# Three one-column constants in one tile: every later buffer 64 bytes lower in a partition

## The chip, the cores and the metric

The kernel runs on one core of one Trainium2 chip. The metric is the device time of one execution in microseconds, as the median of several runs. A core has five engines that take their instructions from queues of their own: TensorE (PE; its weight loads are PEld), VectorE (DVE), ScalarE (ACT), GpSimd (POOL) and SyncE (SP, which here only issues transfers). Transfers between DRAM and the on-chip memory (SBUF, 128 partitions) run on 16 transfer engines that all queues share.

## The reference

One decoding step of a transformer block: attention over a long cache of keys and values for two sequences with one new token each, and then an MLP. All of it is float32.

```python
B, Sq, D = 2, 1, 512
H, Sk, Dh = 32, 8192, 128
def _A_ref(x, k_cache, v_cache, wq, wo):          # caches: (B, H, Sk, Dh)
    q = (x @ wq).reshape(B, Sq, H, Dh).transpose(0, 2, 1, 3)
    scores = jnp.einsum("bhqd,bhkd->bhqk", q, k_cache) * (Dh ** -0.5)
    p = _softmax(scores, axis=-1)
    o = jnp.einsum("bhqk,bhkd->bhqd", p, v_cache)
    return o.transpose(0, 2, 1, 3).reshape(B, Sq, H * Dh) @ wo
def _B_ref(x, w1, b1, w2, b2):                    # w1: (512, 1792)
    y = _layernorm(x, axis=-1)
    h = _gelu(jnp.einsum("bsd,df->bsf", y, w1) + b1)
    return jnp.einsum("bsf,fd->bsd", h, w2) + b2
h = x + _A_ref(_layernorm(x), k_cache, v_cache, wq, wo)
h2 = h + _B_ref(_layernorm(h), w1, b1, w2, b2)
```

Each cache holds 2 x 32 x 8192 x 128 float32 values, 268 MB, and every one of them is read once.

## The kernel before, in words

The 64 pairs of a sequence and a head are taken two heads at a time: 32 iterations `i`, each with one tile of keys and one of values. `load` (L70) brings such a tile, 8 MB, as 128 rows of 64 KB that are contiguous in DRAM, one row to a partition; 64 partitions belong to each of the two heads. The tiles live in the pool `kv`, which has three slots of 64 KB in a partition, so that a load can be issued only when the tile that last used its slot is done with. All these loads, and the weights, are issued on SyncE's queue (L75, L79, L140, L412, L468, L472) in the order of the program.

For the keys of iteration `i`, VectorE multiplies the tile by the query in four chunks of 32 cached positions (`multiply`, L246, in place). The sums over the 128 products are shared out: GpSimd adds the upper half of some positions' products to the lower half (`halve`, L256), VectorE reduces what is left (`sums`, L266), and in the last three iterations ScalarE takes some positions as well (`by_act`, L260). The maximum of the scores (`row_max`, L270) goes through TensorE to all partitions, ScalarE takes the exponentials (`exps`, L291), and TensorE multiplies them by the values of that iteration (`values`, L314) while VectorE is at the keys of the next one. Every second iteration closes two heads: their outputs are summed (`head_sum`, L335), scaled and laid out (`head_out`, L350), and, in groups of rows, multiplied by the output projection, whose rows were loaded into the tile `wog` (`load_wo`, L140, or by an indirect transfer of GpSimd, L145; `turned`, L367). The last two heads' rows of the projection go to `wl`, a view of the query tile `q2` that is free by then (L412).

After the last keys the MLP's weights are loaded into a `kv` slot (`ws`, L468 and L472), w2 in pieces of 7, 4, 2 and 1 rows of 2 KB to a partition; the last values, the rest of the projection, the norm, the MLP and the result follow (L590 and L620 are the MLP's matmuls).

A tile of the `const` pool has its own place in a partition, in the order in which the tiles are made. Each starts at a multiple of 32 bytes, so that a tile with one float32 column takes 32 bytes. The pools `wts` (`wog`), `kv` and `work` lie behind `const` in this order. In the program before, bytes from the start of a partition: `ident` 2176, `orow` 2944, `epst` 7040, `eps2` 7072, `ones` 7104, `onesd` 7616, `ls` 7648, `q2` 11,648, `wog` 15,936, the `kv` slots 24,128, 89,664 and 155,200, the first tile of `work` 220,736; the last ends at 229,312.

`epst` is the bias of the first norm's square root (L197), `eps2` that of the last norm's (L605), and `onesd` holds 1/512, by which a matmul takes the mean of squares (L597).

Of the kernel before, what the change touches and what calls it, by code (L numbers as in the profile page):

```python
# [9 lines left out]
F32 = mybir.dt.float32  # L10
# [6 lines left out]
P = 128  # L17
# [24 lines left out]
def tile_decode_block(ctx: ExitStack, tc: tile.TileContext, x, k, v, wq, wo, w1, b1, w2, b2, out):  # L42
# [14 lines left out]
    const = ctx.enter_context(tc.tile_pool(name="const", bufs=1))  # L57
# [88 lines left out]
            t.rearrange("p r n -> p (r n)"), None, wo_runs, bass.IndirectOffsetOnAxis(index[shut], 0),  # L146
            element_offset=r0 * D, bounds_check=n // r - 1, oob_is_err=False))

    epst = const.tile([P, 1], F32, name="epst")
    nc.vector.memset(epst, EPS)  # L150
    eps2 = const.tile([P, 1], F32, name="eps2")
    nc.vector.memset(eps2, EPS * EPS)
    ones = const.tile([P, P], F32, name="ones")
    nc.vector.memset(ones, 1.0)
    onesd = const.tile([P, 1], F32, name="onesd")
    nc.vector.memset(onesd, 1.0 / D)


# [492 lines left out]
```

## Time and profile before

| what | value |
|---|---|
| median of 3 runs | 1307.6 us (1307.48 to 1307.62) |
| span of the profiled execution, first to last instruction | 1305.9 us (the page gives no other total for it) |
| busy: VectorE, GpSimd, TensorE, ScalarE | 932.7, 494.2, 446.8, 98.6 us |
| read from DRAM | 562.32 MB, 431 GB/s over the span |
| mean granted clock of TensorE | 0.660 |

The page's lines for transfers give, for each queue, the packets, the megabytes, and the time that the packets took as a share of 16 engines' span. A packet here is mostly one contiguous row; 4-byte packets are the signals that a transfer sends when it has landed. The view of windows cuts the span into stretches and gives in its last two columns the share of the 16 transfer engines that packets starting in the stretch took, and GB/s. Where a view says "<-", what stands behind it is what ended the idle time.

### The profile page before, as it was taken

How to read it: one execution, taken by the hardware profiler on the slowest of the kernel's cores; microseconds unless marked ns; L12 is line 12 of the kernel's file. 1: busy time of each engine (PE TensorE's matmuls, PEld its weight loads, DVE VectorE, ACT ScalarE, POOL GpSimd, SP SyncE). 2: the span in 40 equal slices, each digit the busy share in tenths (PEclk: the TensorE clock that was granted, in tenths of full speed). 3: DMA queues.
4: the chain of work that ended last, by engine and by line, in shares of the span. 5: the costliest groups of instructions: out<-in, count | busy, mean ns of one | idle time of the engine just before them, and what ended most of it. 6: DMA issues, size and time to landing. Idle time of an engine off the chain costs nothing.

```text
span 1305.9 us, 7466 instructions
## 1 busy us (share of the span) xinstructions
PE 446.8 (34%) x2934; PEld 130.9 (10%) x2934; DVE 932.7 (71%) x551; ACT 98.6 (8%) x431; POOL 494.2 (38%) x151
## 2 busy tenths in 40 slices
PE   3033313333332334413342232333323334123468
PEld 0001001010010101001010010101001011000113
DVE  3666688757688666787766787666787667797891
ACT  0000000000000000000000000000000000004440
POOL 0433344532344432444332454333444433453330
PEclk9566556766566666656766566666666666566689
DMA  9999999999999999999999999999999999999998
GB/s 418 426 440 428 438 422 444 424 440 426 442 426 440 428 438 428 426 444 430 436 426 438 430 434 436 424 442 424 440 426 432 438 432 436 429 428 429 428 434 351
DMA packets 12727, 561.50 MB, mean 430 GB/s; under 512 B 1568, under 2 KB 1584, under 8 KB 2484
## 3 DMA queue, kind: packets, MB, share of 16 engines
q1 hardware_dynamic: 11968, 557.08, 98.8%
q0 software_dynamic: 720, 3.93, 0.7%
q8 instruction: 23, 0.38, 0.1%
q14 instruction: 12, 0.10, 0.0%
q10 hardware_dynamic: 4, 0.00, 0.0%
HBM read 562.32 MB, written 0.00 MB: 431 GB/s over the span
## 4 chain that ended last, share of the span: by engine, by line
DMA 43%; DVE 24%; issue 14%; PE 12%; POOL 5%; ACT 1%; SPq 0%; POOLq 0%; DVEq 0%
DMA kv<-in_A_k_cache_dram 38%; DVE kv L246 14%; PE so L314 10%; DVE s L266 9%; POOL kv L256 5%; DMA kv<-in_A_v_cache_dram 3%; DMA ws<-in_B_w_dram 1%; ACT pt L291 1%; PE rowacc L367 1%; DVE orow L350 1%; PE sm L280 1%; PE sm L273 0%; DVE gm L277 0%; DVE mx L270 0%; ACT nb L286 0%
## 5 line engine op out<-in xcount | busy, mean ns | idle before, releaser
L246 DVE TENSOR_TENSOR kv<-kv,qps 128x4096 f32<-128x4096 f32 x128 | 562.4, 4415 | 313.8 <-DMA kv<-in_A_k_cache_dram 313.6
L256 POOL TENSOR_TENSOR kv<-kv 128x2048 f32<-128x2048 f32 (+3 forms) x128 | 476.8, 3734 | 754.1 <-DVE kv L246 566.3
L266 DVE TENSOR_REDUCE s<-kv 128x32 f32<-128x2048 f32 (+5 forms) x160 | 325.3, 2066 | 10.9 <-POOL kv L256 10.6
L314 PE MATMUL so<-kv,pt 128*8 128x512 f32 x2048 | 280.8, 709 | 42.7 <-ACT pt L291 37.3
L273 PE MATMUL sm<-ident,mx 128*1 128x128 f32 x32 | 10.9, 340 | 446.0 <-DVE mx L270 446.0
L314 PEld LDWEIGHTS so<-kv,pt 128*8 128x8 f32 x2048 | 56.4, 101 | 239.5 <-issue 194.3
L367 PE MATMUL rowacc<-wog,ot 128*2 128x512 f32 x70 | 50.3, 881 | 64.8 <-DVE ot L365 33.4
L286 ACT ACTIVATE nb<-sm 128x2 f32<-128x2 f32 x32 | 5.5, 172 | 851.4 <-PE sm L280 851.4
L231 PE MATMUL qps<-q,pick 2*64 2x256 f32 x64 | 13.8, 577 | 127.6 <-DVE kv L246 127.6
L273 PEld LDWEIGHTS sm<-ident,mx 128*1 128x1 f32 x32 | 2.5, 79 | 472.5 <-issue 278.0
L358 PE MATMUL sm<-ident,orow 2*128 2x2 f32 x35 | 5.2, 244 | 130.1 <-DVE orow L350 130.1
L320 ACT ACTIVATE ss<-so 128x512 f32<-128x512 f32 x31 | 18.5, 598 | 269.6 <-PE so L314 269.6
L260 ACT ACTIVATE kv<-kv 128x128 f32<-128x128 f32 x114 | 33.5, 295 | 24.2 <-DVE kv L246 21.4
L335 PE MATMUL sm<-ss,selr 128*34 128x128 f32 x240 | 28.7, 273 | 0.0
L291 ACT ACTIVATE pt<-s,nb 64x128 f32<-64x128 f32 x64 | 25.5, 399 | 1.4
L335 PEld LDWEIGHTS sm<-ss,selr 128*34 128x34 f32 x240 | 25.1, 112 | 0.0
L260 ACT ACTIVATION_READ_ACCUMULATOR kv<-kv 128x1 f32 x114 | 21.3, 186 | 0.0
L280 PE MATMUL sm<-gm,ones 1*128 1x2 f32 x64 | 16.6, 326 | 11.9 <-DVE gm L277 11.9
L277 DVE TENSOR_REDUCE gm<-sm 1x2 f32<-1x128 f32 x32 | 8.9, 279 | 16.2 <-PE sm L273 16.2
L231 PEld LDWEIGHTS qps<-q,pick 2*64 2x64 f32 x64 | 5.5, 192 | 136.9 <-DVE kv L246 133.2
L358 PEld LDWEIGHTS sm<-ident,orow 2*128 2x128 f32 x35 | 4.4, 207 | 132.6 <-DVE orow L350 79.9
L367 PEld LDWEIGHTS rowacc<-wog,ot 128*2 128x2 f32 x70 | 6.8, 107 | 97.9 <-issue 64.1
(110 smaller groups left out, 169.2 us busy)
## 6 DMA issues: line engine op xcount, KB each, us to landing
kv<-in_A_k_cache_dram SPq DMA_DIRECT2D x4, 4096.0 KB, 32.9
ws<-in_B_w_dram SPq DMA_DIRECT2D x3, 1792.0 KB, 18.5
kv<-in_A_v_cache_dram SPq DMA_DIRECT2D x1, 4096.0 KB, 33.4
wog<-in_A_wo_dram SPq DMA_DIRECT2D x3, 1024.0 KB
kv<-in_A_v_cache_dram SPq DMA_DIRECT2D x1, 2048.0 KB, 37.9
kv<-in_A_v_cache_dram SPq DMA_DIRECT2D x1, 1536.0 KB, 41.2
ws<-in_B_w_dram SPq DMA_DIRECT2D x1, 1024.0 KB, 17.0
wog<-in_A_wo_dram SPq DMA_DIRECT2D x1, 512.0 KB
```

The source lines that it names most:

```text
L231: nc.tensor.matmul(t[e * HP:(e + 1) * HP, :, b], pick[32 * n:32 * n + B, b, :], rows[:, :, e], start=True, stop=True)
L246: return nc.vector.tensor_tensor(kc, kc, qb, op=ALU.mult)
L256: nc.gpsimd.tensor_tensor(t[:, :, :DH // 2], t[:, :, :DH // 2], t[:, :, DH // 2:], op=ALU.add)
L260: nc.scalar.activation(kt[i][:, j, :], kt[i][:, j, :], AF.Copy, accum_out=ST[i][:, j:j + 1])
L266: nc.vector.tensor_reduce(ST[i][:, a:e], kt[i][:, a:e, :d], axis=AX.X, op=ALU.add)
L273: nc.tensor.transpose(MT[i], mx, ident)
L280: GI[i] = nc.tensor.matmul(GM[i], ones[:1, :], gm, start=True, stop=True)
L291: nc.scalar.activation(ptz[i % 2][ps, :, 4 * e:4 * e + 4], s[ps], AF.Exp, bias=nb[ps, e:e + 1], scale=SCALE, accum_out=LT[m][ps, 32 * e + ...
L314: m = nc.tensor.matmul(so[32 * n:32 * n + 4 * QG], ptz[i % 2][:, u, :], vt[i][:, 4 * u:4 * u + 4, :], start=(u < NG), stop=(u >= NS // 4 - ...
L320: return nc.scalar.activation(SS[i], so2[i % 2], AF.Copy)
L335: nc.tensor.matmul(OP[m], sel_row[:, j, B - 1 - c:B - 1 - c + QR], SS[i - 1 + c][:, j * DH:(j + 1) * DH], start=(c == 0 and j == 0), stop= ...
L367: nc.tensor.matmul(rowacc, t[:, r, :], wo_g[g][:, r, :], start=False, stop=(g == len(groups) - 1 and r == n - 1))
```

## The change

The three tiles `epst`, `eps2` and `onesd` of one column each become the three columns of one tile `small`. The memsets that fill them, and their readers, are as before. By the rule of 32 bytes for a tile, `small` takes 32 bytes where the three took 96. `ones`, which stood between the second and the third, moves 32 bytes down, and all that is made after `onesd`, with the pools behind `const`, moves 64 bytes down.

```diff
-    epst = const.tile([P, 1], F32, name="epst")
+    small = const.tile([P, 3], F32, name="small")
+    epst, eps2, onesd = (small[:, j:j + 1] for j in range(3))
     nc.vector.memset(epst, EPS)
-    eps2 = const.tile([P, 1], F32, name="eps2")
     nc.vector.memset(eps2, EPS * EPS)
     ones = const.tile([P, P], F32, name="ones")
     nc.vector.memset(ones, 1.0)
-    onesd = const.tile([P, 1], F32, name="onesd")
     nc.vector.memset(onesd, 1.0 / D)
```

## The prediction

> **What bounds the kernel now.** I read the page from its busy shares to its transfers, then the queue of the loads, then the chain at the end.
>
> ```profile
> span 1305.9 us, 7466 instructions
> PE 446.8 (34%) x2934; PEld 130.9 (10%) x2934; DVE 932.7 (71%) x551; ACT 98.6 (8%) x431; POOL 494.2 (38%) x151
> DMA  9999999999999999999999999999999999999998
> ...
> DMA packets 12727, 561.50 MB, mean 430 GB/s; under 512 B 1568, under 2 KB 1584, under 8 KB 2484
> ...
> q1 hardware_dynamic: 11968, 557.08, 98.8%
> q0 software_dynamic: 720, 3.93, 0.7%
> q8 instruction: 23, 0.38, 0.1%
> ...
> kv<-in_A_v_cache_dram SPq DMA_DIRECT2D x31, 30.6
> kv<-in_A_k_cache_dram SPq DMA_DIRECT2D x30, 38.4
> ```
>
> No engine is above 71%, but the transfers are: the shares of the queues add up to 98.8 + 0.7 + 0.1 = 99.6% of 16 transfer engines' span, or 1300.7 us of 1305.9. The next rows, stretches of the windows view (the last two columns are the transfers' share and GB/s), show where the rest is: ahead of the first load and behind the last.
>
> ```profile
> 0.00:1.80 1.80, 0.00 (x0) 0.00 (x0) 0.79 (x1) 0.49 (x1) 1.22 (x9) 1.00 0.43 148
> 1.80:1302.00 1300.20, 445.90 (x2918) 130.57 (x2922) 931.67 (x550) 98.08 (x431) 492.93 (x143) 0.66 1.00 432
> 1302.00:1305.90 3.90, 0.86 (x24) 0.33 (x16) 0.29 (x1) 0.00 (x0) 0.00 (x0) 0.88 0.00 1
> ```
>
> Between 1.8 and 1302 us the transfers never rest. The queue is never short of a load either: one is released when the scores' maximum or the last value matmul gives a buffer back, as the waits of SyncE's queue show, and the V loads then take 30.6 us to land.
>
> ```profile
> SPq L75 <- DVE mx L270: 764.5, 28, 29.7
> SPq L75 <- PE sm L301: 175.9, 15, 12.6
> SPq L75 <- PE so L314: 170.4, 15, 13.3
> ```
>
> What a load needs by itself is worked out below (19.4 us). So a V load is issued 30.6 - 19.4 = 11.2 us before its transfer can begin, a K load 38.4 - 19.4 = 19.0 us. That much delay of the computing costs nothing. The chain at the end is transfers too, from the value loads' issue until 1301.75 us, with 1.2 us of computing after that before the result is sent:
>
> ```profile
> 1242.83 42.02 DMA kv<-in_A_v_cache_dram
> 1284.85 0.02 issue
> 1284.87 16.88 DMA ws<-in_B_w_dram
> 1301.75 0.04 issue
> 1301.79 0.64 PE po L620 x16
> ```
>
> So the time is the start, plus bytes and packets through 16 engines, plus a short end. The page gives the profiled execution a span of 1305.9 us and no total of its own; the median of the runs is 1307.6, 1.7 us above the span. I take those 1.7 us as lying around the span and carry them over unchanged.
>
> **The price of a transfer.** To see what an address can change I need the part of a transfer that is not proportional to its bytes. Two rows give it: the page's whole q1 row above (mostly rows of 64 KB), and the last weight pieces, 2 KB and 4 KB rows (1297 to 1302 us). A third window holds two 4-byte packets and nothing else.
>
> ```profile
> q1 hardware_dynamic: 410, 1.63, 80.2%
> ```
>
> ```profile
> q0 software_dynamic: 2, 0.00, 5.6%
> ```
>
> Let a packet cost a, and a kilobyte (1000 B) on one engine b. The whole: 11968 a + 557,080 b = 0.988 x 16 x 1305.9 us = 20,644 us. The small pieces: 410 a + 1630 b = 0.802 x 16 x 5 us = 64.2 us. That gives a = 10.0 ns (give or take 0.5 ns for the rounded megabytes) and b = 36.84 ns, or 27.1 GB/s on an engine and 434 GB/s on 16. A 64 KB row (65.5 x 36.84 + 10) is 2424 ns, and a load of eight rows per engine 19.4 us. As a sum over the kernel: 561.50 MB x 36.84 / 16 = 1292.9 us for bytes and 12,727 x 10.0 / 16 = 8.0 us for packets, together 1300.9 against 1300.7 in the shares. A stretch that was not used fits:
>
> ```profile
> DMA packets 7773, 390.84 MB, mean 433 GB/s; under 512 B 988, under 2 KB 988, under 8 KB 1244
> ...
> q1 hardware_dynamic: 7175, 387.39, 99.2%
> ```
>
> This is 297 to 1200 us: 7175 x 0.010 + 387.39 x 36.84 = 14,343 us by the two prices, 0.992 x 16 x 903 = 14,332 by the row.
>
> The third window is 0.02 us long: 0.056 x 16 x 20 ns = 18 ns for two packets, 9 ns for one of 4 bytes. A packet too small to straddle any boundary thus pays nine tenths of what a 64 KB row pays beyond its bytes.
>
> [...]
>
> **The change part by part.** *The three memsets* stay, with the same shapes and places in the program, and so do the readers of the three columns:
>
> ```profile
> 1.87 0.06 DVE L150 MEMSET epst<- 128x1 f32 x1
> 1.88 0.06 DVE L152 MEMSET eps<- 128x1 f32 x1
> 2.03 0.06 DVE L156 MEMSET onesd<- 128x1 f32 x1
> 4.59 0.29 ACT L197 ACTIVATE lnsd<-lnmv,epst 2x1 f32<-2x1 f32 x1 [1.99 <-DVE lnmv L195]
> 23.34 9.51 PE L216 MATMUL so<-wqs,yT 128*2 128x512 f32 x64 [15.16 <-DMA wqs<-in_A_wq_dram]
> 1290.79 0.22 PE L597 MATMUL so<-onesd,sv 128*32 128x1 f32 x8
> 1293.75 1.71 PE L590 MATMUL so<-ws,ones 128*32 128x448 f32 x16 [0.48 <-DMA ws<-in_B_w_dram]
> ```
>
> One tile for three columns could make the first reader (L197, the square root) wait for all three memsets. The last of them ends at 2.09 us, and L197 starts at 4.59 behind a later VectorE result; behind it stands the query projection, which waits for its weights until 23.3 us. At the other end L597 reads a column written 1288 us earlier, and TensorE then idles 0.48 us for weights at 1293.75: a wait of up to that length is free. Cost 0; without the cover it would be a semaphore wait of some tenths of a microsecond, once.
>
> *The engines' operands.* Every later buffer stands 64 bytes lower; `ones`, between the old second and third column, 32 lower. If a compute instruction cost more or less for that, it would be hidden by the 11.2 us of lead per load:
>
> ```profile
> L246 DVE TENSOR_TENSOR kv<-kv,qps x128: 4399/4414/4423, 42.6 to 1258.8; 128x4096 f32<-128x4096 f32 x128
> L314 PE MATMUL so<-kv,pt x2048: 592/592/1061, 74.9 to 1285.3; 128*8 128x512 f32 x187
> ```
>
> The multiply takes 4399 to 4423 ns (shortest and longest of 128) while transfers write a neighbouring buffer, a spread of 0.5%, so no clash of addresses shows in it. Were all four multiplies of a load 10% slower, that would be 4 x 0.44 = 1.8 us of the 11.2. Cost 0.
>
> *The transfers' destinations.* This is the one term that reaches the end. By the program's allocation before, the three 64 KB slots of `kv` start at byte 24,128 of a partition (94 x 256 + 64) and follow each other by 65,536; `wog` starts at 15,936 (62 x 256 + 64). All of them begin 64 bytes past a multiple of 256, and of 512. After, they start at 24,064 = 47 x 512 and 15,872 = 31 x 512. So nearly all transferred bytes, which went to addresses off by 64, go to addresses that are multiples of 512. The trace has no such row, so its price is bounded from both sides. Packets of 512 B or more are 12,727 - 1568 = 11,159, or 697 per engine; 1 ns on each is 0.70 us of time. The best is that the whole a of 10.0 ns goes: 697 x 10.0 = 7.0 us less (1300.6). The worst is that a row costs as though cut in two, a second a: 7.0 us more (1314.6). The nearest row is the 4-byte packet, whose 9 ns can have nothing to do with the start of a row: that leaves 1.0 ns, give or take 0.5, in which alignment could play a part. I take half, 0.5 ns: 697 x 0.5 = 0.35 us less. A second row speaks the same way: the last 512 KB of `wo` go to `q2`, which starts at 11,648 = 45 x 256 + 128 and so twice as far off, in 256 rows of 2 KB among others (1260 to 1266 us):
>
> ```profile
> q1 hardware_dynamic: 336, 2.49, 99.9%
> ```
>
> By the two prices 336 x 0.010 + 2.49 x 36.84 = 95.1 us against 0.999 x 16 x 6 = 95.9 here, 0.8 us more (0.2 of it from the rounded megabytes), 3 ns on each of the 256. Even if it were all due to the address, the first 64 bytes would be worth no more than that, about 3 x 697 = 2.1 us.
>
> [...]
>
> *Sum.* 0 + 0 - 0.35, on a span of 1305.9: 1305.5; with the 1.7 us around it 1307.2.
>
> **The rivals.** *Faster: both ends of a row cost a whole line.* If each row that starts 64 bytes off writes a partial piece of 256 bytes at its start and another at its end, and pays both in full, it moves 256 bytes too many: 256 x 36.84 = 9.4 ns, 697 x 9.4 = 6.6 us, 1301.0. For it: a is 10.0 ns, near 9.4, and no aligned row stands in this trace to refute it. Against it: the 4-byte packet pays 9 ns, and the row 128 off pays no less. Chance 0.20, with the milder forms that save over 3.7 ns a packet (2.6 us / 697).
>
> [...] Chance 0.14.
>
> *The addresses don't matter, or don't move as said* (the tiles padded to some larger unit): 1307.6, in the same class as the forecast.
>
> **How the numbers follow.** What a measurement of this kernel can tell from no change is about 0.2%, 2.6 us. [...] The range for 8 in 10 reaches on the faster side to 1302.0, which takes in most of that rival, and stops at 1310.2 on the slower side, leaving out its 0.14.
>
> **What would show it.** Right: q1 holds about 98.8% of the span, the window 297 to 1200 us keeps its 433 GB/s, and a and b come out again as 10 ns and 36.8 ns. [...] If instead the share in the middle falls under 0.99, the queue ran dry, and a wait that I called free was not. The multiply's 4414 ns and TensorE's 592 ns should stand unchanged; if they move by tenths of a microsecond, an address matters to engines, though not to the time.

## The result, and the profile after

The changed kernel takes 1304.53 us (median of 12 runs, 1304.31 to 1305.24), the kernel before 1307.61 (12 runs beside them): 3.08 us less, a ratio of 0.9977 with a 95% interval of 0.9969 to 0.9985. That lies inside the range of the prediction (1302.0 to 1310.2), 2.7 us under its forecast of 1307.2, and 0.5 us beyond the 2.6 us that were to separate "the same" from "faster".

The page of the changed kernel has the same instructions and the same packets, in a shorter span:

```profile
span 1302.7 us, 7466 instructions
PE 451.7 (35%) x2934; PEld 132.7 (10%) x2934; DVE 932.7 (72%) x551; ACT 98.6 (8%) x431; POOL 494.1 (38%) x151
...
DMA packets 12727, 561.50 MB, mean 431 GB/s; under 512 B 1568, under 2 KB 1584, under 8 KB 2484
...
q1 hardware_dynamic: 11968, 557.08, 98.9%
```

VectorE is busy to the same 932.7 us, and the queue of the loads still fills the span. The windows view has the same two edges, 1.8 us at the start and 3.9 us at the end, and a middle that is shorter by 3.2 us (1297.0 for 1300.2):

```profile
0.00:1.80 1.80, 0.00 (x0) 0.00 (x0) 0.79 (x1) 0.49 (x1) 1.22 (x9) 1.00 0.32 112
1.80:1298.80 1297.00, 450.80 (x2918) 132.40 (x2922) 931.66 (x550) 98.11 (x431) 492.86 (x143) 0.65 1.00 433
1298.80:1302.70 3.90, 0.86 (x24) 0.34 (x16) 0.29 (x1) 0.00 (x0) 0.00 (x0) 0.88 0.01 2
```

In the stretch from 297 to 1200 us the transfers moved 391.62 MB, against 390.84 before, again without a pause:

```profile
DMA packets 7785, 391.62 MB, mean 434 GB/s; under 512 B 988, under 2 KB 988, under 8 KB 1244
...
q1 hardware_dynamic: 7187, 388.17, 99.3%
```

That is 0.2% more per microsecond, and the kernel is 0.24% faster. The lead of the loads (issue to landing, from the transfers view) is all but unchanged, and so are the engines' instructions:

```profile
kv<-in_A_v_cache_dram SPq DMA_DIRECT2D x31, 30.2
kv<-in_A_k_cache_dram SPq DMA_DIRECT2D x30, 38.3
```

```profile
L313 PE MATMUL so<-kv,pt x2048: 592/592/1061, 74.8 to 1282.6; 128*8 128x512 f32 x187
L245 DVE TENSOR_TENSOR kv<-kv,qps x128: 4397/4414/4422, 42.5 to 1257.8; 128x4096 f32<-128x4096 f32 x128
```

The chain at the end consists of the same pieces, only earlier (the columns are start and length in us), and the shared tile cost no wait: behind the matmul that reads it, TensorE's weight load still idles for the MLP's weights (0.37 us; 0.76 before).

```profile
1240.62 41.52 DMA kv<-in_A_v_cache_dram
1282.13 0.02 issue
1282.15 16.41 DMA ws<-in_B_w_dram
1298.56 0.04 issue
1298.61 1.09 PE po L619 x24
```

```profile
1288.07 0.22 PE L596 MATMUL so<-small,sv 128*32 128x1 f32 x8
...
1290.64 0.16 PEld L589 LDWEIGHTS so<-ws,ones 128*32 128x32 f32 x8 [0.37 <-DMA ws<-in_B_w_dram]
```

The trace keeps the duration of every packet. Counted by size, for the queues of the loads (q0 and q1) and the most frequent sizes, they tell what the views only sum up:

```
row of      packets (both kernels)   mean ns before   after    shortest before = after
4 B         1566                        9.1             9.1       9
2 KB         514                       86.0            84.7      84
4 KB         384                      161.1           159.0     159
8 KB         992                      315.2           311.5     309
32 KB        640                     1219.8          1215.0    1213
64 KB       7936                     2424.8          2420.5    2418 (a single one in some kernels: 2415)

64 KB rows:   up to 2418   2419 to 2423   2424 to 2432   longer
before           18%           55%            25%          2%
after            96%            3%             1%          1%
those that start from 300 us on, up to 2418: before 6%, after 99.5%
```

The shortest packet of each size has not changed by a nanosecond. Before, over half of the 64 KB rows took 1 to 5 ns more than the shortest (most often 2), and a quarter of them mostly 7 to 9 ns more; after, nearly all are as short as the shortest. In the first 100 us the two kernels are still alike, with 51% and 57% of the rows at the shortest; they part after that. Over all packets an engine's transfers add up, on average, to 1302.25 us before and 1299.19 after: 3.06 us, which is the whole gain of 3.08. The 64 KB rows make 2.12 us of it.

### The profile page after: what moved, and what is told of

Its sections match the earlier page's. It is cut to its first block, busy times and chain, and to the rows that moved or that the text cites. A ratio compares the mean times of both kernels' runs of the same rounds, so it can differ in the third digit from the quotient of the medians.

```text
span 1302.7 us, 7466 instructions
## 1 busy us (share of the span) xinstructions
PE 451.7 (35%) x2934; PEld 132.7 (10%) x2934; DVE 932.7 (72%) x551; ACT 98.6 (8%) x431; POOL 494.1 (38%) x151
## 4 chain that ended last, share of the span: by engine, by line
DMA 42%; DVE 23%; issue 14%; PE 13%; POOL 5%; ACT 1%; SPq 0%; POOLq 0%; DVEq 0%
DMA kv<-in_A_k_cache_dram 38%; DVE kv L245 14%; PE so L313 10%; DVE s L265 8%; POOL kv L255 5%; DMA kv<-in_A_v_cache_dram 3%; PE rowacc L366 1%; DMA ws<-in_B_w_dram 1%; ACT pt L290 1%; DVE orow L349 1%; PE sm L279 1%; PE sm L272 0%; DVE gm L276 0%; DVE mx L269 0%; ACT nb L285 0%
## 5 line engine op out<-in xcount | busy, mean ns | idle before, releaser
L366 PE MATMUL rowacc<-wog,ot 128*2 128x512 f32 x70 | 53.4, 930 | 64.8 <-DVE ot L364 33.4
```

The source lines that it names most:

```text
L366: nc.tensor.matmul(rowacc, t[:, r, :], wo_g[g][:, r, :], start=False, stop=(g == len(groups) - 1 and r == n - 1))
```

## The experiments

The theory after the result, called A in the expectations: a row whose destination starts off a boundary is stretched. Its rivals: the gain comes from the constants and operands of the engines (B); 32 bytes are the natural unit of a transfer, and only the engines' order in time shifted (C); it comes from a difference of phase between source and destination (D); it needs the engines' own traffic (E), or several transfer engines at once (F). The "offset" below is the distance of `wog`, the `kv` slots and `work` from the last multiple of 512 bytes. All ratios are to the kernel before on the same chip, whose median was 1307.6 us for the whole kernels and 1307.7 for the loads alone.

**Constants low, big buffers back.**

```diff
     sq = const.tile([P, DC, B], F32, name="sq")
+    const.tile([P, 16], F32, name="pad")
```

> The changed kernel with an unused 64-byte tile behind the last constant: all constants keep their new, lower places, and only wog, the three kv slots and the work pool go back to 64 bytes past a multiple of 512. Theory A (a row whose destination starts off the boundary is stretched, whoever else uses the memory): all of the gain goes, 1307.6 us, ratio 1.000 to before. Theory B (the constants and operands of the engines stand better): the gain stays, 1304.5, ratio 0.998.

Measured: 1307.7 us (11 runs), ratio 1.000 (0.9991 to 1.0009). The whole gain is gone, and the window of 297 to 1200 us is back at its old rate:

```profile
span 1305.7 us, 7466 instructions
```

```profile
DMA packets 7775, 390.97 MB, mean 433 GB/s; under 512 B 988, under 2 KB 988, under 8 KB 1244
```

**Big buffers low, constants back.**

```diff
-    junk = const.tile([P, 2], F32, name="junk")
+    tail = const.tile([P, 6], F32, name="tail")
+    junk = tail[:, 0:2]
...
-    wsum = const.tile([P, QG], F32, name="wsum")
+    wsum = tail[:, 2:4]
...
-    wmean = const.tile([P, QG], F32, name="wmean")
+    wmean = tail[:, 4:6]
```

> The other half: the three constants are separate tiles as before, and three result columns behind q2 (junk, wsum, wmean) share one tile instead, so that every constant up to q2 stands where it stood and only wog, kv and work stand 64 bytes lower, on multiples of 512. Theory A: the whole gain, 1304.5 us, ratio 0.998. Theory B: 1307.6, ratio 1.000.

Measured: 1304.67 us, ratio 0.9977 (0.9968 to 0.9986), with the three constants as separate as before:

```profile
span 1302.6 us, 7466 instructions
```

```profile
DMA packets 7785, 391.62 MB, mean 434 GB/s; under 512 B 988, under 2 KB 988, under 8 KB 1244
```

Theory B is out. The tile of three columns has no part in the gain; the 64 bytes by which the big buffers moved have all of it.

**Other offsets.** The changed kernel with padding of 32, 256 and 128 bytes, that is, 8, 64 and 32 numbers. At 256 and 128, six small tiles of `work` also get one buffer instead of two, for room (not shown):

```diff
     sq = const.tile([P, DC, B], F32, name="sq")
+    const.tile([P, 8], F32, name="pad")
```

> The changed kernel with 32 bytes of padding: wog, kv and work start 32 past a multiple of 512. Theory A with any offset alike: 1307.6 us, ratio 1.000. Theory A in proportion to the offset (half of 64): about 1306, ratio 0.999. Theory C (a half, 32 off, is itself the natural unit of a transfer, so that only the order in time of the engines shifts): 1304.5.

> The changed kernel with 256 bytes of padding (six one-use tiles of work get one buffer instead of two to make room): wog, kv and work start 256 past a multiple of 512. If the boundary that counts is 256 bytes: 1304.5 us, ratio 0.998. If it is 512: 1307.6, ratio 1.000.

> The changed kernel with 128 bytes of padding (six one-use tiles of work get one buffer instead of two to make room): wog, kv and work start 128 past a multiple of 512. At 0 and 256 the 64 KB rows took 2418 ns almost without exception, at 32 and 64 most took 2420 to 2428. Theory A with 256 as the unit: slow again, 1307.6 us, ratio 1.000. With 128 as the unit: 1304.6, ratio 0.998. [...]

Measured: 1308.27 us at 32 (ratio 1.0005, 0.9996 to 1.0014), 1304.87 at 256 (0.9978, 0.9969 to 0.9987), 1307.54 at 128 (1.0000, 0.9991 to 1.0009). So 0 and 256 are alike (1304.53 and 1304.87), and 32, 64 and 128 are alike within 0.7 us: among these starts, what counts for the time is whether it is a multiple of 256, not how far it is off. The 64 KB rows of these runs, by the packets of the trace, agree:

```
offset           up to 2418   2419 to 2423   2424 to 2432   longer   mean ns   median of the runs
0 (changed)         96%            3%             1%           1%     2420.5     1304.53
256                 97%            2%             1%           1%     2421.0     1304.87
32                   8%           63%            27%           2%     2425.8     1308.27
64 (before)         18%           55%            25%           2%     2424.8     1307.61
128                 26%           47%            25%           3%     2425.9     1307.54
```

These shares include the start of the run, where the offset makes little difference. Of the rows that start from 300 us on, 99.5% and 99.6% are at the shortest at 0 and 256, and 0.6%, 6% and 20% at 32, 64 and 128, with means of 2424.2, 2423.4 and 2423.4 ns.

The second and third expectation of the 32-byte run, a cost in proportion (about 1306) and 32 bytes as the natural unit (C, 1304.5), fail against its 1308.27.

**The source moved instead.** Keys and values read 64 bytes further on, with the destinations of before and of after. These kernels compute on a shifted cache, so only their times count:

```diff
-        rows = src[b, QG * m:QG * m + QG].rearrange("h (p j) d -> (h p) j d", j=NS)
+        at = (b * H + QG * m) * SK * DH + (16 if i < NI - 1 else 0)
+        rows = src.rearrange("b h s d -> (b h s d)")[at:at + P * NS * DH].rearrange("(p j d) -> p j d", j=NS, d=DH)
```

> The kernel before, with every row of keys and values but those of the last iteration read 64 bytes further on in DRAM (the attention is computed on a cache shifted by 16 numbers, and the last 16 of a head come from the next). Source and destination then stand equally far past a multiple of 256. Theory A (the destination alone counts): 1307.6 us, ratio 1.000. Theory D (the pieces read and the pieces written have to be cut at the same places, and a difference of phase costs): the gain, 1304.6, ratio 0.998. [...]

> The changed kernel with the same shift of the source by 64 bytes: destination on the boundary, source 64 past it. [...] Theory D: the phases differ again, 1307.6, ratio 1.000.

Measured: 1307.64 us with both 64 off (ratio 1.0001, 0.9992 to 1.0010), 1304.82 with the source alone off (0.9980, 0.9971 to 0.9989). Theory D is out: an equal phase does not help, a different one does not hurt. Of the two, the destination counts (1307.64 and 1304.82 with the same source). With the source alone off, the median is 0.3 us above the changed kernel's (1304.82 against 1304.53), within the noise, as theory A has it; 97% of its 64 KB rows take up to 2418 ns, against 96% with the source where it was. That the caches themselves begin at a multiple of 256 in DRAM is taken for granted here; no run shows it.

**Slots with different offsets.**

```diff
-        t = kv.tile([P, NS, DH], F32, name="kv", tag="kv")
+        t = kv.tile([P, NS * DH + 16], F32, name="kv", tag="kv")[:, :NS * DH].rearrange("p (s d) -> p s d", d=DH)
```

> The changed kernel with kv slots that are 64 bytes longer (six one-use tiles of work get one buffer instead of two to make room), so that the three slots start 0, 64 and 128 past a multiple of 512 and successive loads differ. Theory A as a property of each row: loads into the first slot take 2418 ns a row, those into the second 2420 to 2427, and about two thirds of the gain go, 1306.6 us, ratio 0.999. If the stretching needs several off-boundary rows in flight together (the 256 rows that go to q2 did not stretch in the changed kernel although they start 64 off): rows of the first slot stretch too, or those of the others do not.

Measured: 1306.05 us, ratio 0.9988 (0.9979 to 0.9997): half of the gain went, where a pure property of the row was to take two thirds. By the order of the loads, each third one goes to the same slot; the slots come up in the order 0, 128, 64. Of the rows of keys and values to the slot at 0, 87% took 2418 ns, to the slot at 64, 39%, and to the slot at 128, 86%. The first two go the way of a property of each row. The third does not: with every slot at 128 (above) only 26% were as short. So a row's time also depends on the rows around it; in which way, these runs do not show.

**Loads alone.** No computing; each slot is given back when one number of it was copied. Offsets 64, 0 and 16:

```diff
-        for c in range(NC):
-            ...
+        for src in (k, v):
+            t = load(src, i, [(0, NS)])
+            nc.vector.tensor_copy(out_row[:, 0:1], t[:, 0, 0:1])
```

> Loads alone: the query weights and the 64 tiles of keys and values go through the three kv slots as in the kernel before, each slot given back as soon as one number of its tile was copied, and nothing is computed; the slots start 64 past a multiple of 512. 545 MB at the price per byte and packet give about 1258 us. Theory A (the transfers stretch one another or themselves): about 520 rows per engine, 4 to 5 ns each, 2.2 us more than the same loads on the boundary. Theory E (it needs the engines' own traffic in the memory): no difference from them, and rows of 2418 ns.

> The same loads alone with the slots on multiples of 512. Rows of 2418 ns by either theory; 2.2 us less than 64 off by theory A, the same by theory E.

> [...] If only the cutting into pieces counts, as at 32 and 64: about 2 to 3 us more than on the boundary. [...]

Measured (4 runs each): 1266.98 us at 64, 1264.82 at 0, 1267.67 at 16; the first two differ by 2.16 us, as expected of theory A. The total came out 7 to 10 us above the 1258 worked out ahead; the packets themselves add up to 1259.5 us an engine at 0 and 1261.4 at 64, and the rest lies around them. VectorE is busy 1% of the time here (4.77 of the 600 us from 600 to 1200 us, GpSimd 0), so theory E is out. The sliced rates of the two pages (64 first, then 0) show the difference, as far as whole GB/s can: most slices of the middle read 431 at 64 and 432 at 0.

```profile
GB/s 412 416 431 433 452 441 431 431 431 431 431 431 431 431 431 431 445 447 433 429 431 431 433 431 431 431 431 431 431 450 441 431 433 431 433 431 431 431 431 365
```

```profile
GB/s 405 446 440 436 432 432 432 432 432 432 432 432 432 432 432 432 438 450 440 430 432 432 434 432 432 432 432 432 432 436 448 440 434 432 432 434 432 432 432 365
```

In the window of 600 to 1200 us both moved 4464 packets and 260.05 MB; what differs is the time that these took, 64 first:

```profile
q1 hardware_dynamic: 4464, 260.05, 100.2%
```

```profile
q1 hardware_dynamic: 4464, 260.05, 100.0%
```

From 196 us on, all but two of some 7000 rows at offset 0 take 2418 ns. Earlier they do not: in the first 100 us only 66% do, and 56% at offset 64, so there the offset hardly shows. At 64, all but two of the rows between 100 and 158 us take 2418; from 158 us on they take mostly 2420 and 2427, and from about 200 us in nearly the same shares load after load. At 16, most take 2422 and 2429 from about 100 us on; the time is 2.85 us above the one at 0 (1267.67 against 1264.82), inside the 2 to 3 us expected.

**Few engines.** Loads alone again, in stages of 127 rows and fewer and a last one of 128 (`load` is rewritten to take the number of rows and the offset, not shown):

```diff
+    for rows, off, times in ((127, 0, 1), (127, 1, 1), (122, 1, 2), (124, 1, 4), (120, 1, 6), (128, 1, 12)):
+        nc.sync.dma_start(gate, x.rearrange("b s d -> (b s) d")[:, 0:1])
+        for _ in range(times):
+            load((k, v)[n % 2], n, rows, off)
+            n += 1
+        nc.vector.tensor_copy(out_row[:B, 1:2], gate)
```

> [...] The first stage (127 rows, one engine) goes to a slot on a multiple of 512, all later ones to slots 64 past it. Theory F (a row off the boundary is stretched only when other engines write at the same time): rows of 2418 ns with one engine, off the boundary or on it, and 2420 to 2427 ns only from some number of engines on, at the latest with 16. [...]

Measured: 1926.48 us (2 runs). The stages did not stay apart (the second load was issued at 148 us, in the middle of the first, and a later stage at 449 us, in the middle of the second), and overlapping rows took up to twice as long (up to 5 us). The first two loads are still clean: their rows come one after another. Up to 449 us one engine works, as the share of 6.2%, one sixteenth, shows for 310 to 449 us:

```profile
DMA packets 57, 3.74 MB, mean 27 GB/s; under 512 B 0, under 2 KB 0, under 8 KB 0
...
q1 hardware_dynamic: 57, 3.74, 6.2%
```

The durations of this engine's rows in their order, from the packets of the trace (ns; the count in brackets where the same one repeats):

```
on the boundary, rows 11 to 127:    2418 (all but 2475 once and 2422 twice)
64 past it, from 310 us on:         2418 (33), 2425, 2420, 2420, 2420, 2427, 2420, 2420, 2420, 2427, 2420, 2420, 2420, 2427, ...
```

Theory F is out: a single engine shows the stretch, in a strict pattern of three rows with 2 ns more and one with 9 ns more, 15 ns in four rows or 3.8 ns a row. On the boundary it doesn't appear in 117 rows (of the first ten, the very first took 3316 ns and most others 2420). But the pattern sets in only after 33 rows that were as short as on the boundary, and the load on the boundary came first; so this run alone does not show that it is the destination that keeps a single engine's rows short. The later stages, where loads on several engines overlapped, say nothing about the offset.

What is shown: the gain is the transfers' own (3.06 us of packets for 3.08 us of time), it comes from big destinations on a multiple of 256 bytes (1304.53 and 1304.87 us at 0 and 256, 1307.54 to 1308.27 at 32, 64 and 128), and neither a moved source (1304.82) nor the engines' own work (2.16 us between the loads alone) is needed for it; the stretch itself needs no second transfer engine (2420 and 2427 ns on one). What stays open is why the offset shows only after 100 to 300 us, why rows 128 off keep short between others (86%, against 26% with every slot at 128), and so what inside a transfer makes the stretch. No version among these beats the changed kernel: at offsets 0 and 256 practically all rows that start from 300 us on (99.5% and 99.6%) are as short as the shortest.

## Why the prediction was right, and where its sum was off

The measured 1304.53 us lies inside the stated range, but outside the neighbours of the forecast itself (1305.0 to 1310.2, the likeliest case's own range, which had a chance of 0.66). The range took it in because its faster end was set at 1302.0 for the sake of the faster rival. The sum foresaw a gain of 0.35 us, about a ninth of the one that came. So the account of what bounds the kernel was right; that the total came so near owes something to a range that was wide against the effect.

*What bounds the kernel* held. The transfers set the time (share 1.00 from 1.8 to 1298.8 us), the loads' lead hid the computing (30.2 and 38.3 us to land, for 19.4 of transfer), and a saving in packet time came through one for one: 3.06 us of packets, 3.08 us of time.

*The memsets and readers: 0.* Right, by the idle 0.37 us before the weights and by the run with the constants separate, which is as fast.

*The engines' operands: 0.* Right. The multiply's median is 4414 ns as before, and moving the constants alone changes nothing (ratio 1.000).

*The transfers' destinations: 0.35 us.* This is the term that was mis-sized; it measured 3.06. The step that failed is "the nearest row is the 4-byte packet ... that leaves 1.0 ns in which alignment could play a part". The 4-byte packet is indeed the same before and after (9.1 ns), and so is the shortest packet of each size: neither shows any alignment in the fixed cost, as argued. The stretch lies elsewhere. It is larger on longer rows, though far from in proportion: in the means, 1.3 ns on 2 KB, 2.1 on 4 KB, 3.7 on 8 KB, 4.8 on 32 KB and 4.3 on 64 KB (the 384 rows of 14 KB, not in the table, are out of line with 8.3). A fit with one price per packet and one per byte spreads such a thing over both, and I searched for it in the one alone. The price per byte I took as full, and that was not shown: the trace before has no big row on a boundary to compare with. The mean 64 KB row came down from 2424.8 to 2420.5 ns, or 0.2%, and that is just the size of what was looked for. Over the 697 packets per engine the saving is 3.06 us / 697 = 4.4 ns, beyond the 3.7 that I had named as the point from which "faster" decides.

The same two prices for the changed kernel, from its page and its last weight pieces (1293.8 to 1298.8 us),

```profile
q1 hardware_dynamic: 423, 1.72, 83.6%
```

come out as a = 8.4 ns and b = 36.82 ns per kilobyte, against 10.0 and 36.84. With 0.5 ns of rounding in a, this says that something became cheaper and not what; the spread of the packets' durations, which the sums hide, says it at once.

*The row 128 off* (256 rows to `q2`) was read as about 3 ns on each, worth at most 2.1 us on all rows; the gain of 3.06 us lies above that bound. By their packets these rows are on average 3.3 ns above the shortest, 84 ns, but four of them (109 to 226 ns) make 1.5 of that, and 155 of the 256 are at the shortest. In the changed kernel they still start off the boundary, 64 past it (11,584 = 45 x 256 + 64), and 244 of them take 84 ns. So this row could not price an address by itself: its small excess went when the big destinations around it moved.

*The rivals.* The faster one, a whole line too many at both ends of a row, has the size of the longest stretch (9.4 ns worked out; 2427 against 2418 measured), but only about one row in four shows it (25% at 2424 to 2432 ns before), and a size alone does not show that this mechanism makes it. So its milder form, put at over 3.7 ns a packet, came true, and its full 1301.0 did not. Together they had a chance of 0.20; the measured interval for the ratio, 0.9969 to 0.9985, spans the 0.2% edge. The slower side, which had 0.14, did not come: on the boundary the shortest 64 KB row takes the 2418 ns it took before, and 96% of the rows take no more, against 18%. That the addresses don't matter, the core of the 0.66, was wrong, though by little more than the edge.

## What to carry to other kernels

Where transfers fill the span, as they did here, a few nanoseconds on each row are the time: 4.3 ns on the mean 64 KB row, with what the shorter rows gave, made 3.06 us of packets and 3.08 us of time. So try big tiles that start at a multiple of 256 bytes in a partition (1304.5 and 1304.9 us here, against 1307.5 to 1308.3 off it), and look where small tiles ahead of them push them, since a harmless tidying of constants gained 0.2% here, and 64 bytes of padding lost it again (1307.7). When a price per packet and per byte is fitted, look at the spread of single packets of one size too: where the shortest and the usual one differ (2418 and 2420 ns here), that is reserve that no sum shows. And when the question is 0.2%, a price per byte fitted on big rows that all start 64 bytes off does not tell what a row on the boundary costs.

## What the hardware showed unexpectedly

Rows of 64 KB to destinations at multiples of 256 bytes took 2418 ns in 95 to 97% of the cases wherever all slots stood so, with the source moved or not, and in over 99% of those that started from 300 us on. From 300 us on, at 16, 32 and 64 bytes off, the usual row took 2422, 2421 and 2420 ns and about a fifth 2429, 2428 and 2427: among these three a smaller distance cost a little more, not less. At 128 off there is no usual row, and a fifth stay at the shortest. In the first 100 us of the runs on 16 engines 42 to 69% of the rows took up to 2418 ns, and the offset hardly sorts them. On one engine the pattern was three short stretches and one long in every four rows, and it set in only after 33 rows.

The few packets that bring the program's instructions (queue `q8`, 23 in a run) follow the loads: they took 938 to 940 ns on average in the four kernels with all big destinations on a multiple of 256, and 1046 to 1072 in the five with all of them off it and the one with mixed slots. None of this was expected, and none of it is explained here.
